# A two-layer MLP's first product by one level of Strassen's scheme, on one core

## The chip, the cores and the metric

One core of a Trainium2 chip runs the whole kernel. The metric is the device time of one execution in microseconds. The engines are TensorE (PE, its weight loads PEld), VectorE (DVE), ScalarE (ACT), GpSimd (POOL) and SyncE (SP), which here only issues DMAs.

## The reference

q, k, v are 8 x 8 x 576 x 64 (batch, head, token, feature) and phi is 8 x 8 x 576 x 32. A softmax of phi over the tokens condenses k and v to 32 memories per head; each token attends to them. The heads side by side give x, 4608 x 512. Two MLPs follow:

```python
x = attention(q, k, v, phi)                    # 4608 x 512
r = np.maximum(x @ w_in1, 0); x = (s * r * r + b) @ w_out1
r = np.maximum(x @ w_in2, 0); out = (r * r) @ w_out2
```

Each w_in is 512 x 2048 and each w_out 2048 x 512. The weights are 64-bit floats in DRAM, the rest 32-bit.

## The kernel before

**Products in three parts.** Each operand is split in two float32r tiles, the cast of it and what the cast leaves, and a product is three matmuls: high by high, high by low, low by high. A cast is an ACT instruction and the remainder a DVE subtraction.

**The first MLP** (lines 568 to 661) runs with the attention over the 8 batches in half-batches of 288 tokens. A step is one half-batch and one of 16 tiles of 128 hidden features: `h1` (line 447) makes 6 matmuls of 288 columns, `x1` (line 469) 12. `h1` is two steps ahead. The attention is a generator of which `slot` runs a piece after so many slots. The result goes to the DRAM tiles `x1d`, transposed (features by tokens).

**Weights.** `narrow` (line 102) makes 32-bit floats of a piece of 64-bit weights: a multiplication on ACT (line 121) and three bit operations on DVE (lines 122 to 125). From step `SPILL` (66), every eighth step takes one of 16 pieces of w_in2 and w_out2 and writes it to DRAM (`wi2d`, `wo2d`, 0.5 MB each, line 132), at a priority behind the step's own work.

**The hand-over.** In the last batch `early` (line 551) opens the buffers of the second MLP, splits half of w_in2 (line 528) and loads and splits the first 512 tokens of x (line 532).

**The second MLP** (lines 666 to 737) runs over 9 blocks of 512 tokens and 16 hidden tiles f, with `h2` (line 672) two steps ahead. `h2` makes 12 matmuls of 512 columns into one bank of `ps_h` (4 feature tiles by 3, line 678), then ACT takes the Relu out of the bank, DVE squares it, ACT casts it and DVE subtracts (lines 683 to 686). Then 4 x 3 matmuls with wo2, 512 columns each, add to four banks of `ps_a` that stay for the block (line 726). `piece` (line 698) splits the other half of w_in2, and wo2, two pieces a step during the first block. At f = 4 the next block of x is loaded, at f = 8 split. After the last f each bank is copied (ACT or DVE) and stored.

The order of the work is the program's, as a list scheduler places it by priority on each engine's queue; each queue runs in order. A tile's buffer is given out again once all that use it are done.

Of the kernel before, what the change touches and what calls it, by code (L numbers as in the profile page):

```python
# [20 lines left out]
def memory_attention_then_two_relu2_mlps(  # L21
# [36 lines left out]
    NB2 = 512  # L58
    NBLK2 = NT // NB2
# [15 lines left out]
    ps_a = ctx.enter_context(tc.tile_pool(name="ps_a", bufs=4, space=PSUM))  # L75
    ps_h = ctx.enter_context(tc.tile_pool(name="ps_h", bufs=2, space=PSUM))
    ps_m = ctx.enter_context(tc.tile_pool(name="ps_m", bufs=2, space=PSUM))
    dram = ctx.enter_context(tc.tile_pool(name="dram", bufs=1, space=DRAM))
    x1d = [dram.tile([P, ND, XG], F32, name=f"x1d{i}") for i in range(NT // XG)]
    wi2d = [dram.tile([P, ND, 512], F32, name=f"wi2d{n}") for n in range(NV)]  # L80
# [10 lines left out]
    def narrow_later(src, kind, dst):  # L91

        narrow_todo.append((src.rearrange("(i p) f -> p i f", i=2), kind, dst))

    def narrow_load(n=1, later=30):
        for src, kind, dst in [narrow_todo.pop(0) for _ in range(min(n, len(narrow_todo)))]:
            with tc.high_priority(-later) if later else ExitStack():
                t = w64_p.tile([P, 2, 512], I64, tag="t", name="wt")
                nc.sync.dma_start(t, src)
            loaded.append((t, kind, dst))  # L100

    def narrow(n=1):
# [5 lines left out]
        for _ in range(n):  # L108
# [5 lines left out]
            with tc.high_priority(-100 if kind == "spill" else -10):  # L114
# [5 lines left out]
                with tc.issue_after(st["act"].ins) if kind == "spill" else ExitStack():  # L120
                    nc.scalar.mul(xf, hw.bitcast(F32), 2.0 ** -112)  # L121
# [9 lines left out]
                elif kind == "spill":  # L131
                    nc.sync.dma_start(dst[0], xf)

# [386 lines left out]
    wi2, xs, early_pools, early_split = [], {}, [], []  # L520
# [11 lines left out]
    def load_x(i):  # L532
        xs_p = early_pools[1]
        t0 = i * NB2
        xh = xs_p.tile([P, ND, NB2], F32R, tag="xh", name="xh")
        xl = xs_p.tile([P, ND, NB2], F32R, tag="xl", name="xl")
        xs[i] = xh, xl
        x = xs_p.tile([P, ND, NB2], F32, tag="x", name="x", bufs=1)
        a = t0
        while a < t0 + NB2:  # L540
            n = min(t0 + NB2 - a, XG - a % XG)
            nc.sync.dma_start(x[:, :, a - t0:a - t0 + n], x1d[a // XG][:, :, a % XG:a % XG + n])
            a += n

        def split():
            for d in range(ND):
                nc.scalar.copy(xh[:, d], x[:, d])
                nc.vector.tensor_tensor(out=xl[:, d], in0=x[:, d], in1=xh[:, d], op=ALU.subtract)
        return split

    def early():
        p2 = ctx.enter_context(tc.tile_pool(name="w2", bufs=1))
        early_pools.extend([p2, ctx.enter_context(tc.tile_pool(name="xs", bufs=2))])
        wi2.extend(p2.tile([P, ND, 2, 512], F32R, name=f"wi2_{n}") for n in range(NV // 2))
        held = []

        def piece(n, d):
            def go():
                if held:
                    held.pop(0)()  # L560
                if n is not None:
                    held.append(split_w(wi2[n][:, d], wi2d[n][:, d]))
                elif d == 0:
                    held.append(load_x(0))
            return go
        early_split.extend([piece(n, d) for n in range(NV // 2) for d in range(ND)] + [piece(None, 0), piece(None, 1)])
# [55 lines left out]
    for i in range(-AHEAD, len(steps)):  # L622
        if i >= 0:
# [13 lines left out]
            if i == SPILL:  # L637
                for n in range(NV):
                    for d in range(0, ND, 2):
                        narrow_later(w_in2[d * P:d * P + 2 * P, n * 512:n * 512 + 512], "spill", [wi2d[n][:, d:d + 2]])  # L640
# [8 lines left out]
        if b == B - 1 and early_split:  # L649
# [13 lines left out]
    right.close()  # L663


    late_p = ctx.enter_context(tc.tile_pool(name="late", bufs=1, side="right"))
    wi2.extend(late_p.tile([P, ND, 2, 512], F32R, name=f"wi2_{n}") for n in range(NV // 2, NV))
    wo2 = late_p.tile([P, NF, 2, DM], F32R, name="wo2")
    gp = ctx.enter_context(tc.tile_pool(name="gp2", bufs=4, side="right"))
    tmp = ctx.enter_context(tc.tile_pool(name="tmp2", bufs=2, side="right"))  # L670

    def h2(i, f):
        hps = ps_h.tile([P, 512], F32, tag="h", name="hps")
        n = 0
        for d in range(ND):
            w = wi2[f // 4][:, d, :, (f % 4) * P:(f % 4) * P + P]
            for wi, xi in ((0, 0), (0, 1), (1, 0)):
                nc.tensor.matmul(hps[:, :NB2], lhsT=w[:, wi], rhs=xs[i][xi][:, d],  # L678
                                 start=(n == 0), stop=(n == 3 * ND - 1))
                n += 1  # L680
        r = tmp.tile([P, NB2], F32, tag="r", name="r")
        g = [gp.tile([P, NB2], F32R, tag=f"g{i}", name=f"g{i}") for i in range(2)]
        nc.scalar.activation(r, hps[:, :NB2], AF.Relu)  # L683
        nc.vector.tensor_tensor(out=r, in0=r, in1=r, op=ALU.mult)  # L684
# [4 lines left out]
    outv = out.rearrange("(b p j) d -> b j p d", b=B, j=J)  # L689
    steps = [(i, f) for i in range(NBLK2) for f in range(NF)]  # L690

    pieces = [(wo2[:, f], wo2d[f // 2][:, f % 2]) for f in range(NF)]
    more = [(wi2[n][:, d], wi2d[n][:, d]) for n in range(NV // 2, NV) for d in range(ND)]
    for n, p in enumerate(more):
        pieces.insert(3 + 2 * n, p)
    held = []
# [6 lines left out]

    for _ in range(3):
        piece()
    for i in range(-AHEAD, len(steps)):
        if i + AHEAD < len(steps):
            gs[i + AHEAD] = h2(*steps[i + AHEAD])
        if i < 0:
            continue  # L710
        blk, f = steps[i]
        if held or pieces:
            piece()
            piece()
        if f == 4 and blk + 1 < NBLK2:
            x_split = load_x(blk + 1)
        if f == 8 and blk + 1 < NBLK2:
            x_split()
        if f == 0:
            acc = [ps_a.tile([P, 512], F32, tag="a", name="oacc") for _ in range(NB2 // P)]  # L720
            o = [ost.tile([P, ND * NB1], F32, tag="o", name="oo") for _ in range(2)]
            o = [o[t // 2][:, t % 2 * DM:t % 2 * DM + DM] for t in range(NB2 // P)]
        g = gs.pop(i)
        for t in range(NB2 // P):
            for n, (xi, wi) in enumerate(((0, 0), (0, 1), (1, 0))):
                nc.tensor.matmul(acc[t], lhsT=g[xi][:, t * P:t * P + P], rhs=wo2[:, f, wi],  # L726
                                 start=(f == 0 and n == 0), stop=(f == NF - 1 and n == 2))
            if f == NF - 1:
                if t % 2:
                    nc.vector.tensor_copy(o[t], acc[t])  # L730
                else:
                    nc.scalar.copy(o[t], acc[t])

                for z in range(2):
# [33 lines left out]
```

## Time and profile before

| what | value |
|---|---|
| time, median of 3 runs | 1573.13 us (1572.85 to 1573.28) |
| span of the profiled execution | 1572.9 us |
| TensorE busy | 1544.8 us, 98% |
| DVE busy | 672.7 us, 43% |
| ACT busy | 692.9 us, 44% |
| DMA | 118.06 MB, mean 75 GB/s |
| second MLP, first to last matmul | 771.47 to 1568.13 us |

The span runs from the first to the last instruction of one profiled execution; its own time is that span, and no other time is given for it. A busy TensorE only says that some matmul was in flight, so how dense the matmuls are is read from the chain in time (how long so many took).

### The profile page before, as it was taken

The numbers are of one execution on the slowest core, as the hardware profiler recorded it, in microseconds if no ns is written. First come the engines' busy times: TensorE is split into PE (matmuls) and PEld (weight loads), VectorE is DVE, ScalarE is ACT, GpSimd is POOL, SyncE is SP. The second block draws the span as 40 slices with busy tenths as digits, with TensorE's granted clock in tenths as the row PEclk, the third lists the DMA queues.
The fourth block names the chain that finished last, engine by engine and source line by source line (L and its number), as shares of the span: only waits on it lengthen the run. The fifth ranks groups of instructions, "written<-read, shape, count | busy, mean of one in ns | idle before, by whom it ended". The sixth has DMA issues, their size and how long they took to land.

```text
span 1572.9 us, 25769 instructions
## 1 busy us (share of the span) xinstructions
PE 1544.8 (98%) x10816; PEld 1343.2 (85%) x10816; DVE 672.7 (43%) x1168; ACT 692.9 (44%) x1467; POOL 1.0 (0%) x7
## 2 busy tenths in 40 slices
PE   5899999999999999999999999999999999999998
PEld 4789989999898999989988888888888888888887
DVE  6985545556555564443353223232323223232222
ACT  4677555656656665576543222222322222222221
POOL 0000000000000000000000000000000000000000
PEclk8999999999999999999999999999999999999999
DMA  9764414344153522032130101020200101010100
GB/s 298 229 193 141 124 59 123 94 154 144 62 180 98 176 82 77 26 97 69 56 108 27 27 1 54 0 54 0 54 1 27 27 1 54 1 28 0 27 1 27
DMA packets 105300, 118.06 MB, mean 75 GB/s; under 512 B 42208, under 2 KB 82144, under 8 KB 105184
## 3 DMA queue, kind: packets, MB, share of 16 engines
q1 hardware_dynamic: 104864, 115.89, 23.8%
q8 instruction: 85, 1.39, 0.4%
q10 hardware_dynamic: 320, 0.52, 0.1%
q14 instruction: 31, 0.25, 0.1%
HBM read 86.77 MB, written 29.62 MB: 74 GB/s over the span
## 4 chain that ended last, share of the span: by engine, by line
PE 95%; DVE 2%; DMA 1%; ACT 1%; issue 0%; SPq 0%; ACTq 0%; DVEq 0%
PE hps L678 25%; PE oacc L726 25%; PE acc L474 25%; PE hps L457 13%; PE vps L426 2%; PE sp L322 1%; PE kvs L239 1%; PE qps L307 1%; PE pp L350 1%; DMA kv<-in_v_dram 0%; DMA wt<-in_moe_w_in_dram 0%; DMA wt<-in_moe_w_out_dram 0%; DVE wx L123 0%; DVE pm L194 0%; ACT wx L121 0%
## 5 line engine op out<-in xcount | busy, mean ns | idle before, releaser
L474 PE MATMUL acc<-g,wo 128*128 128x288 f32 (+1 forms) x3072 | 464.6, 297 | 0.5 <-DVE wo L130 0.3
L474 PEld LDWEIGHTS acc<-g,wo 128*128 128x128 f32 x3072 | 422.4, 188 | 23.3 <-ACT r L464 11.7
L726 PE MATMUL oacc<-wo,g 128*128 128x512 f32 x1728 | 419.6, 392 | 0.0
L726 PEld LDWEIGHTS oacc<-wo,g 128*128 128x128 f32 x1728 | 324.3, 188 | 73.4
L678 PE MATMUL hps<-xh,wi 128*128 128x512 f32 x1152 | 384.1, 394 | 0.0
L684 DVE TENSOR_TENSOR r<-r 128x512 f32<-128x512 f32 x144 | 99.7, 693 | 444.6 <-ACT r L683 444.6
L683 ACT ACTIVATE r<-hps 128x512 f32<-128x512 f32 x144 | 86.0, 597 | 460.9 <-PE hps L678 460.9
L457 PE MATMUL hps<-pt,vp 128*128 128x288 f32 x1536 | 257.1, 300 | 1.5 <-DVE pt L360 0.8
L678 PEld LDWEIGHTS hps<-xh,wi 128*128 128x128 f32 x1152 | 216.1, 188 | 49.5
L457 PEld LDWEIGHTS hps<-pt,vp 128*128 128x128 f32 x1536 | 220.2, 190 | 12.4 <-issue 7.5
L678 PE MATMUL hps<-xl,wi 128*128 128x512 f32 x576 | 225.4, 391 | 0.0
L466 DVE TENSOR_TENSOR g<-r,g 128x288 fp32r<-128x288 f32 x256 | 116.6, 456 | 230.7 <-ACT g L465 228.1
L463 ACT ACTIVATE r<-hps 128x288 f32<-128x288 f32 x256 | 105.2, 411 | 182.2 <-PE hps L457 179.8
L686 DVE TENSOR_TENSOR g<-r,g 128x512 fp32r<-128x512 f32 x144 | 99.6, 692 | 84.5 <-ACT g L685 84.5
L685 ACT CAST g<-r 128x512 fp32r<-128x512 f32 x144 | 89.4, 621 | 94.9 <-DVE r L684 93.8
L678 PEld LDWEIGHTS hps<-xl,wi 128*128 128x128 f32 x576 | 108.1, 188 | 25.1
L464 ACT ACTIVATE r<-r 128x288 f32<-128x288 f32 x256 | 113.7, 445 | 7.0
L465 ACT CAST g<-r 128x288 fp32r<-128x288 f32 x256 | 110.5, 432 | 6.3
L432 DVE TENSOR_TENSOR vp<-vps,vp 128x512 fp32r<-128x512 f32 x64 | 41.6, 686 | 13.0 <-ACT vp L431 12.5
L431 ACT CAST vp<-vps 128x512 fp32r<-128x512 f32 x64 | 34.6, 587 | 15.8 <-PE vps L426 15.7
L121 ACT ACTIVATE wx<-wt 128x1024 f32<-128x1024 f32 x32 | 36.8, 1150 | 10.4 <-DMA wt<-in_moe_w_in_dram 8.2
L123 DVE SCALAR_TENSOR_TENSOR wx<-wt,wx 128x1024 int32<-128x1024 int32 x32 | 39.2, 1224 | 0.8
(224 smaller groups left out, 681.1 us busy)
## 6 DMA issues: line engine op xcount, KB each, us to landing
wt<-in_moe_w_in_dram SPq DMA_DIRECT2D x16, 1024.0 KB, 6.1
wt<-in_moe_w_out_dram SPq DMA_DIRECT2D x16, 1024.0 KB, 6.0
q<-in_q_dram SPq DMA_DIRECT2D x72, 128.0 KB, 3.3
x1d<-xo SPq DMA_DIRECT2D x16, 576.0 KB, 3.5
kv<-in_k_dram SPq DMA_DIRECT2D x23, 384.0 KB, 4.6
kv<-in_v_dram SPq DMA_DIRECT2D x23, 384.0 KB, 5.1
out_dram<-oo SPq DMA_DIRECT2D x68, 128.0 KB, 2.3
x<-x1d SPq DMA_DIRECT2D x6, 1024.0 KB, 5.4
```

The lines of the kernel that those rows point to most:

```text
L457: nc.tensor.matmul(hps[:, :NB1], lhsT=w[:, wi], rhs=pt[xi][:, hp, t0:t0 + NB1], start=(i == 0), stop=(i == 5))
L463: nc.scalar.activation(r[:, :NB1], hps[:, :NB1], AF.Relu)
L464: nc.scalar.activation(r[:, :NB1], r[:, :NB1], AF.Square)
L465: st["act"] = nc.scalar.copy(g[0][:, :NB1], r[:, :NB1])
L466: st["dve"] = nc.vector.tensor_tensor(out=g[1][:, :NB1], in0=r[:, :NB1], in1=g[0][:, :NB1], op=ALU.subtract)
L474: nc.tensor.matmul(acc[d][:, :n], lhsT=wo1[:, f, wi, d * P:d * P + P], rhs=g[xi][:, :n], start=(first and i == 0), stop=(store is not None ...
L678: nc.tensor.matmul(hps[:, :NB2], lhsT=w[:, wi], rhs=xs[i][xi][:, d], start=(n == 0), stop=(n == 3 * ND - 1))
L683: nc.scalar.activation(r, hps[:, :NB2], AF.Relu)
L684: nc.vector.tensor_tensor(out=r, in0=r, in1=r, op=ALU.mult)
L685: nc.scalar.copy(g[0], r)
L686: nc.vector.tensor_tensor(out=g[1], in0=r, in1=g[0], op=ALU.subtract)
L726: nc.tensor.matmul(acc[t], lhsT=g[xi][:, t * P:t * P + P], rhs=wo2[:, f, wi], start=(f == 0 and n == 0), stop=(f == NF - 1 and n == 2))
```

## The change

x @ w_in2 is computed on halves of its three dimensions: 512 features in two halves, 2048 hidden features in two, and a pair of token halves of 384. Seven products of halves replace eight. The sums that they need are made once for the weights and once per pair for x:

- `combine` takes a narrowed piece of w_in2 (all 512 features, 128 columns of each hidden half), makes four sums by DVE, splits the seven operands by ACT and DVE, and writes both parts of all seven to DRAM (`wcd[u]`, 1.84 MB), for 8 units u. It takes the place of 8 of the 16 pieces written every eighth step; each is loaded by four DMAs.
- `load_x` loads 768 tokens of x; its seven steps make the sums and split them, for the first pair in the last batch, later in the pair before.
- `load_unit` streams the weights of one unit from DRAM in two DMAs, into two buffers each, for every pair again.
- `unit` makes the seven products of one unit, 6 matmuls of 384 columns each, in three banks: product 0 into a, 1 into b, 2 on top of a, 3 into c, 4 on top of a, 5 on top of c, 6 on top of a. ACT copies the banks after 0, 2 and 3; DVE adds those copies to the banks after 1, 4 and 5, and clamps and squares. The first token half goes on to wo2 at once, as six groups of three 512-column matmuls, one behind each product of the next unit. The second half is stored in 16 tiles `rd`.
- After the eight units of a pair the 16 tiles are cast (`ready`, two ahead) and taken to wo2, three groups each; the groups of the last two tiles go into the next pair's first unit.
- The three PSUM pools close after the first MLP, and one pool of 8 banks takes their place. wo2 still loads by `piece`, twice per unit.

```diff
+    TP = 384
+    NPAIR = NT // (2 * TP)
+    NU = NF // 2
...
+    wcd = [dram.tile([P, 7, 2, 2, P], F32, name=f"wcd{u}") for u in range(NU)]
...
+                if kind == "combine":
+                    flat = t.rearrange("p i f -> p (i f)")
+                    for d in range(ND):
+                        nc.sync.dma_start(flat[:, d * 2 * P:d * 2 * P + 2 * P].rearrange("p (h c) -> p h c", h=2), src[d])
...
+    def combine(xf, dst):
...
+        q4 = xf.rearrange("p i f -> p (i f)").rearrange("p (d h c) -> p d h c", d=ND, h=2)
+        a11, a12, a21, a22 = [q4[:, 2 * kh:2 * kh + 2, fh, :] for fh in range(2) for kh in range(2)]
+        sums = wst.tile([P, 4, 2, P], F32, tag="x", name="ws")
+        s2, s1, s3, s4 = [sums[:, i] for i in range(4)]
+        for out, in0, in1, op in ((s1, a21, a22, ALU.add), (s2, s1, a11, ALU.subtract),
+                                  (s3, a11, a21, ALU.subtract), (s4, a12, s2, ALU.subtract)):
+            nc.vector.tensor_tensor(out=out, in0=in0, in1=in1, op=op)
+        first = w64_p.tile([P, 4, 2, 2, P], F32R, tag="t", name="wc0")
+        second = w64_p.tile([P, 3, 2, 2, P], F32R, tag="t", name="wc1")
+        plain = q4[:, :, 0, :].rearrange("p (e k) c -> p e k c", e=2)
+        for w, part, of in ((first, slice(0, 2), plain), (first, slice(2, 4), sums[:, 0:2]),
+                            (second, slice(0, 2), sums[:, 2:4]), (second, 2, a22)):
+            nc.scalar.copy(w[:, part, 0], of)
+            nc.vector.tensor_tensor(out=w[:, part, 1], in0=of, in1=w[:, part, 0], op=ALU.subtract)
+        nc.sync.dma_start(dst[:, 0:4], first.bitcast(F32))
+        nc.sync.dma_start(dst[:, 4:7], second.bitcast(F32))
...
+    def load_unit(n):
...
+        for i, (a, b) in enumerate(((0, 4), (4, 7))):
+            t = wc_p.tile([P, b - a, 2, 2, P], F32, tag=f"wc{i}", name=f"wc{i}", bufs=2)
+            nc.sync.dma_start(t, wcd[n % NU][:, a:b])
+            ring[n, i] = t.bitcast(F32R)
...
+        b11, b12, b21, b22 = [x[:, 2 * kh:2 * kh + 2, th * TP:th * TP + TP] for kh in range(2) for th in range(2)]
...
+        def split(e, of):
+            xc = xs_p.tile([P, 2, 2, TP], F32R, tag=f"xc{e}", name=f"xc{e}")
+            nc.scalar.copy(xc[:, 0], of)
+            nc.vector.tensor_tensor(out=xc[:, 1], in0=of, in1=xc[:, 0], op=ALU.subtract)
...
+            t1 = less(b12, b11)
+            split(3, t1)
+            yield
+            t2 = less(b22, t1)
+            split(2, t2)
...
+    psx.close()
...
+    ps = ctx.enter_context(tc.tile_pool(name="ps", bufs=8, space=PSUM))
...
+        def product(e, to, start):
+            n = 0
+            for k in range(2):
+                for wi, xi in ((0, 0), (0, 1), (1, 0)):
+                    nc.tensor.matmul(to[:, :TP], lhsT=w[e // 4][:, e % 4, wi, k], rhs=xc[e][:, xi, k],
+                                     start=(start and n == 0), stop=(n == 5), skip_group_check=True)
+                    n += 1
+            return to[:, :TP]
...
+        def added(t, of, to):
+            nc.vector.tensor_tensor(out=t, in0=of, in1=to, op=ALU.add)
+            nc.vector.scalar_tensor_tensor(out=t, in0=t, scalar=0.0, in1=t, op0=ALU.max, op1=ALU.mult)
+
+        p1 = copied(product(0, a, True))
+        yield
+        r = tmp.tile([P, TP], F32, tag="r", name="r")
+        added(r, product(1, b, True), p1)
+        low = cast(r)
+        yield
+        u2 = copied(product(2, a, False))
+        yield
+        c = bank("pc")
+        p5 = copied(product(3, c, True))
+        yield
+        added(rd[NU + u], product(4, a, False), p5)
+        yield
+        added(rd[u], product(5, c, False), u2)
+        yield
+        r = tmp.tile([P, TP], F32, tag="r", name="r")
+        nc.scalar.activation(r, product(6, a, False), AF.Relu)
+        nc.vector.tensor_tensor(out=r, in0=r, in1=r, op=ALU.mult)
+        high = cast(r)
+        groups.extend(block(p, 0, u, low, u == 0, False))
+        groups.extend(block(p, 0, NU + u, high, False, u == NU - 1))
...
+            if n + 1 < NPAIR * NU and n > 0:
+                load_unit(n + 1)
+            if u == 4 and p + 1 < NPAIR:
+                part = load_x(p + 1)
+            for w, _ in enumerate(unit(p, u)):
+                take()
+                if w in (1, 4) and (held or pieces):
+                    piece()
...
+        take(3)
+        for f in fs:
+            ready(f + 2)
+            if f % 2 and p + 1 < NPAIR:
+                next(part, None)
+            if f < NF - 2 or p + 1 == NPAIR:
+                take(6 if f == 0 else 3)
```

## Rows read from the trace of the kernel before

**Rows 1.** The page: busy time of the engines; clock granted in 40 slices.

```profile
PE 1544.8 (98%) x10816; PEld 1343.2 (85%) x10816; DVE 672.7 (43%) x1168; ACT 692.9 (44%) x1467; POOL 1.0 (0%) x7
...
PEclk8999999999999999999999999999999999999999
```

**Rows 2.** The page: chain that ended last, by engine, by line.

```profile
PE 95%; DVE 2%; DMA 1%; ACT 1%; issue 0%; SPq 0%; ACTq 0%; DVEq 0%
PE hps L678 25%; PE oacc L726 25%; PE acc L474 25%; PE hps L457 13%; PE vps L426 2%; PE sp L322 1%; PE kvs L239 1%; PE qps L307 1%; PE pp L350 1%; DMA kv<-in_v_dram 0%; DMA wt<-in_moe_w_in_dram 0%; DMA wt<-in_moe_w_out_dram 0%; DVE wx L123 0%; DVE pm L194 0%; ACT wx L121 0%
```

**Rows 3.** Windows, second MLP: stretch, length, engines' busy us, PEclk, DMA share, GB/s.

```profile
771.30:859.90 88.60, 88.60 (x387) 72.20 (x386) 41.35 (x63) 36.17 (x63) 0.00 (x0) 1.00 0.26 80
859.90:948.40 88.50, 88.50 (x386) 72.02 (x385) 25.82 (x39) 22.65 (x38) 0.00 (x0) 1.00 0.09 24
```

**Rows 4.** Chain in time, second MLP: start us, us, engine, tile, line, count.

```profile
771.47 8.18 PE hps L678 x36
...
804.43 2.75 PE hps L678 x12
...
809.93 2.80 PE hps L678 x12
812.74 2.76 PE oacc L726 x12
...
1559.92 8.21 PE oacc L726 x36
```

**Rows 5.** Chain in time, first MLP.

```profile
412.37 0.80 PE hps L457 x6
413.17 1.59 PE acc L474 x12
...
474.30 0.39 PE acc L474 x3
```

**Rows 6.** Groups by form, ACT and DVE: busy us, mean ns of one, idle before.

```profile
L465 ACT CAST g<-r 128x288 fp32r<-128x288 f32 x256 | 110.5, 432 | 6.3
...
L685 ACT CAST g<-r 128x512 fp32r<-128x512 f32 x144 | 89.4, 621 | 94.9 <-DVE r L684 93.8
...
L221 DVE TENSOR_TENSOR ph<-ph,t 128x384 f32<-128x384 f32 x24 | 11.9, 548 | 1.1 <-PE t L216 1.1
...
L314 ACT COPY qT<-qps 128x384 f32<-128x384 f32 x23 | 10.9, 474 | 5.2 <-PE qps L307 5.1
```

**Rows 7.** Timeline where the second MLP starts: start us, us, instruction, idle before.

```profile
771.60 1.13 ACT L528 CAST wo<-wx 128x512 fp32r<-128x512 f32 x2
...
772.25 1.29 DVE L529 TENSOR_TENSOR wo<-wx,wo 128x512 fp32r<-128x512 f32 x2 [0.16 <-ACT wo L528]
```

**Rows 8.** Groups by form, narrowing the weights: busy us, mean ns.

```profile
L123 DVE SCALAR_TENSOR_TENSOR wx<-wt,wx 128x1024 int32<-128x1024 int32 x32 | 39.2, 1224 | 0.8
...
L121 ACT ACTIVATE wx<-wt 128x1024 f32<-128x1024 f32 x32 | 36.8, 1150 | 10.4 <-DMA wt<-in_moe_w_in_dram 8.2 <-DMA wt<-in_moe_w_out_dram 2.2
...
L122 DVE TENSOR_SCALAR wx<-wx 128x1024 int32<-128x1024 int32 x32 | 22.0, 692 | 13.6 <-ACT wx L121 13.1
```

**Rows 9.** Window at the kernel's start, columns as in rows 3.

```profile
0.00:40.00 40.00, 24.19 (x301) 19.16 (x302) 26.09 (x46) 17.56 (x41) 0.95 (x7) 0.87 0.92 298
```

**Rows 10.** The page: DMA issues, KB each, us to landing.

```profile
x<-x1d SPq DMA_DIRECT2D x6, 1024.0 KB, 5.4
...
x<-x1d SPq DMA_DIRECT2D x2, 768.0 KB, 5.5
```

**Rows 11.** Window in which w_in2 is narrowed, columns as in rows 3.

```profile
262.00:440.00 178.00, 177.83 (x1720) 166.52 (x1719) 100.67 (x187) 112.19 (x260) 0.00 (x0) 1.00 0.40 126
```

**Rows 12.** Timeline of batch 3's k and v loads.

```profile
347.84 0.50 SPq L177 DMA_DIRECT2D kv<-in_v_dram  x1
...
350.90 0.91 PE L239 MATMUL kvs<-kv,e 64*32 64x128 f32 x47 [0.17 <-DMA kv<-in_v_dram]
```

**Rows 13.** The page: weight loads of the first MLP's second product.

```profile
L474 PEld LDWEIGHTS acc<-g,wo 128*128 128x128 f32 x3072 | 422.4, 188 | 23.3 <-ACT r L464 11.7
```

More of the change, by code (lines that the diff above doesn't have):

```diff
@@ L539, in load_x @@
+    def load_x(p):
+        xs_p = early_pools[0]
+        t0, t1 = p * 2 * TP, (p + 1) * 2 * TP
+        x = xs_p.tile([P, ND, 2 * TP], F32, tag="x", name="x")
         a = t0
-        while a < t0 + NB2:
-            n = min(t0 + NB2 - a, XG - a % XG)
+        while a < t1:
+            n = min(t1 - a, XG - a % XG)
             nc.sync.dma_start(x[:, :, a - t0:a - t0 + n], x1d[a // XG][:, :, a % XG:a % XG + n])
             a += n
[L545 to L548, printed above, removed]
@@ L569, in memory_attention_then_two_relu2_mlps @@
+        return steps()
+    def early():
+        early_pools.append(ctx.enter_context(tc.tile_pool(name="w2", bufs=1)))
+        part = load_x(0)
+        load_unit(0)
+        load_unit(1)
+        early_split.extend([lambda: next(part, None)] * 7)
     load_phi(0)
@@ new lines, in memory_attention_then_two_relu2_mlps, with block, group, go @@
+    accs = {}
+    def block(p, half, f, g, first, last):
+        def group(t):
+            def go():
+                if first:
+                    accs[half, t] = bank("oacc")
+                acc = accs[half, t]
+                gg = g() if callable(g) else g
+                for n, (xi, wi) in enumerate(((0, 0), (0, 1), (1, 0))):
+                    nc.tensor.matmul(acc, lhsT=gg[xi][:, t * P:t * P + P], rhs=wo2[:, f, wi],
+                                     start=(first and n == 0), stop=(last and n == 2))
+                if last:
+                    store(p, half, t, acc)
+            return go
+        return [group(t) for t in range(TP // P)]
@@ new lines, in memory_attention_then_two_relu2_mlps, with store @@
+    room = []
+    def store(p, half, t, acc):
+        if t != 1:
+            room[:] = [ost.tile([P, ND * NB1], F32, tag="o", name="oo")]
+        o = room[0][:, t % 2 * DM:t % 2 * DM + DM]
+        if t % 2:
+            nc.vector.tensor_copy(o, acc)
+        else:
+            nc.scalar.copy(o, acc)
+        for z in range(2):
+            grp = ((2 * p + half) * TP + t * P) // 64 + z
+            eng = nc.scalar if (z and p == NPAIR - 1 and half) else nc.sync
+            eng.dma_start(outv[grp // J, grp % J], o[64 * z:64 * z + 64])
@@ L698, in piece @@
+    held, split_of = [], {}
+    pieces = [(wo2[:, f], wo2d[f // 2][:, f % 2]) for n in range(NU) for f in (n, NU + n)]
     def piece():
@@ L702, in piece, with take @@
             held.pop(0)()
+    def take(n=1):
+        for _ in range(min(n, len(groups))):
+            groups.pop(0)()
     for _ in range(3):
         piece()
[L706 to L734, printed above, removed]
-                    grp = (blk * NB2 + t * P) // 64 + z
-                    eng = nc.scalar if (z and blk == NBLK2 - 1) else nc.sync
-                    eng.dma_start(outv[grp // J, grp % J], o[t][64 * z:64 * z + 64])
```

129 lines of the change are left out of this document (70 added, 59 removed).

## The prediction

> **What bounds the kernel now.** I read the page from the top. TensorE is busy 98% of the span at full granted clock [rows 1], but a busy TensorE need not be a full one, so the chain of waits comes next: 95% of the path to the end is matmuls, and half of it is the second MLP, in equal parts x @ w_in2 (line 678) and g @ w_out2 (line 726) [rows 2]. Then that stage by itself: in windows of one 512-token block, 88.5 us long, TensorE is busy 88.5, ACT 22.7, DVE 25.8, DMA a tenth; the clock is 1.00, that is its 2.4 GHz level. In the first block wo2 and half of wi2 are still read and split, DMA at three times the share, and it takes 88.6 us: nothing on another engine shows [rows 3]. The chain in time gives the price of a matmul. It runs from 771.47 to 1568.13 without a hole: 796.66 us for 2 x 1728 matmuls of 512 columns, 230.5 ns each. Line 726 takes 2.76 us for 12, and 8.21 for 36 at the end (2.74); line 678 takes 2.75 or 2.80 for 12 [rows 4]. I put line 726 at 2.755, thus 144 x 2.755 = 396.7 us, and line 678 at the other 400.0 us. So whatever takes columns from TensorE here is worth its full time, as long as nothing else gets late.
>
> **Part 1, the products.** Removed: 9 x 16 x 12 = 1728 matmuls of 512 columns. Added: 6 pairs x 8 units x 7 products x 6 = 2016 of 384. Columns fall by exactly 1/8 (884,736 to 774,144); matmuls rise by 288. No row has a 384-column matmul, so I bound it. In the first MLP, 18 matmuls of 288 columns take 0.80 + 1.59 us, 132.8 ns each, and three alone to a bank 0.39, so short groups cost nothing extra [rows 5]. The line through 132.8 at 288 and 230.5 at 512 (0.436 ns a column, 7 ns fixed) gives 174.7 ns at 384. Ends: 384/512 of 229.2 is 171.9, 384/288 of 132.8 is 177.1. I take the line, since 384 lies between two measured widths. 2016 x 174.7 = 352.2 us (346.6 to 357.0), against 400.0: **-47.8 us** (-53.4 to -43.0).
>
> The Trainium skill, TensorE: Matmul & The Clock Gate, section Back-to-back issue gap, gives N/2.4 + 2.5 ns for an isolated warm matmul: 215.8 at 512 and 162.5 at 384, and a gain of 45.3 us. The rows are 7% above it at 512 and 8% at 288 (122.5 by the page), so I stay with the line.
>
> Line 726 becomes groups of three matmuls of the same 512 columns, still 1728: no change.
>
> **Part 2, the engines behind the products.** Of the ACT and DVE work in the second MLP nothing is on the path while TensorE stays dense; its cover is the unit, 42 x 174.7 + 18 x 229.6 ns (2.755 us / 12) = 11.47 us. ACT: four reads of a 384-column bank at 0.474 us (the COPY of that shape) and two casts at 0.51 (between 0.432 at 288 and 0.621 at 512): 2.9 us. DVE: three adds, three clamp-and-squares, one square, two subtractions, nine at 0.548: 4.9 us [rows 6]. Neither is half full. What counts is the hand-over of a bank. Bank a holds products 0, 2, 4, 6, bank c holds 3 and 5, and each may be added to only after its reader is done. The tightest is product 4: ACT copies bank a after product 2, but on ACT's queue that copy stands behind the cast of the low half, which waits for two DVE operations on product 1. Counted from the end of product 1, with at most 0.16 us for a signal, a subtraction's wait on its cast [rows 7]: DVE from 0.16 to 1.26, cast from 1.42 to 1.93, copy to 2.40, seen by TensorE at 2.57. Product 4 starts after three groups of 0.69 and products 2 and 3 at 1.05, at 4.17. Slack 1.6 us. The others are products 2, 5 and 6, which wait for one read of about 0.5 us with a product and two groups between: 1.05 + 1.38. So zero, while the groups stand between.
>
> They don't in the very first unit, when no group exists yet. There, too, ACT and DVE have just stored the last x1 tile and split two pieces of wo2 for 1.13 and 1.29 us [rows 7], and the accumulators are one new pool over the three old ones, which can hold product 0 until the last store is read. Product 2 and product 4 then come up some 0.5 us short each: **+1 us** (0 to 3).
>
> At the end of a pair TensorE has three groups, 2.07 us, before it needs the cast of the first stored tile. If that cast is issued behind the last unit's own chain (read 0.47, square 0.55, cast 0.51, then itself 0.51 and 0.55) it comes at 2.6 to 3.1. It need not be, since those tiles are ready long before and ACT is idle there. Six pairs, 0 to 1 us each: **+2 us** (0 to 6). In that phase 9 matmuls (2.07 us) cover one cast and one subtraction per tile, begun two tiles ahead, and every second tile brings a step of the next pair's splits (768 columns, a cast and one or two subtractions), below the rows of 1024 columns, 1.15 on ACT and 1.22 on DVE, or twice that on DVE [rows 8]; the dearest pair of tiles asks 2 x 0.55 + 2.45 = 3.6 of DVE's 4.1 us: nothing.
>
> **Part 3, the weight stream.** A unit needs 7 x 2 x 2 x 128 floats per partition, 1.84 MB, 48 times, two DMAs each; removed are 16 loads of wi2 pieces and the loads of x in blocks of 512 tokens. Per 11.47 us that is 160 GB/s. The start of the kernel moves 298 GB/s over 40 us [rows 9]; the nearest single transfers take 5.4 us (1024 KB) and 5.5 (768 KB) [rows 10]. Even one after the other they fit, 10.9 of 11.47, and each has the ring's second buffer: the first DMA of unit n+1 can go when product 3 of unit n-1 is done, some 15 us early. The x load of a pair (1.57 MB at unit 4, on the same SP queue) costs 11 us so counted, and the last pair-phase without loads (33 us) pays it back. On SP the output stores stand between loads only once per half. Zero, from 0 to what rival B says. Its cover gone, each late microsecond counts 48 times.
>
> **Part 4, the first MLP.** Eight pieces that before cost ACT 1.15 and DVE 3.1 us (1.224 twice and 0.69) [rows 8] get four sums, four casts and four subtractions: about +2.3 on ACT and +4.2 on DVE each, and write 1.84 MB instead of 0.5 MB. In 262 to 440 us, where they run, DVE is busy 101 of 178 us and ACT 112; +34 and +18 leave a quarter of each free, under a TensorE that is full [rows 11]. But the k and v loads are just in time there: issued at 347.84, waited for 0.17 us at 350.90 [rows 12]. They share SP's queue with the new stores and with three more load issues per piece. A store that sits ahead of them for 5.4 us at both batches of that stretch is the upper end. **+2 us** (0 to 11).
>
> The end is as before: the copy and the store of the last tile.
>
> **The sum.** The span, 1572.9 us, is 0.2 below the median of the three runs, 1573.13, so I count from the median: 1573.1 - 47.8 + 1 + 2 + 2 = 1530.3, say 1530.
>
> **Rivals.**
> A, slower: the hand-overs are exposed. If a bank's reader and its next writer come to stand side by side on TensorE, by the order that the scheduler writes or because ACT's copies queue behind casts, each of the four per unit costs a copy and a signal each way, 0.47 + 2 x 0.16 = 0.79 us: 48 x 4 x 0.79 = 152 us, 1682. It decides at (47.8 - 5) / 48 = 0.9 us per unit; with 0.5 it gives 1554. Against it: 1.6 us of slack at the tightest place, and ACT and DVE under half full. 0.11, of that 0.05 beyond the break-even.
> B: the weights come late. It needs under 160 GB/s; at 140, 13.1 us per unit, 48 x 1.6 = 79 us, 1609. For it: 160 GB/s has to be held where this stage now moves 24 [rows 3]. Against: 298 at the start [rows 9]. 0.04.
> C: the combining holds up the first MLP, 11 us instead of 2: 1539. For it, the k and v loads without slack; against, the free quarter of DVE. 0.10.
> D: the price is per matmul, not per column. If every weight load were paid in full, 288 more at 188 ns are +54.1 against -48.2 for the columns (110,592 at 0.436), with the 5 us of waits 1584. It decides at (48.2 - 5) / 288 = 150 ns a matmul. The row speaks against it: a whole matmul of 288 columns takes 132.8 ns, less than its 188 ns load [rows 5, 13]. 0.01. The Trainium skill, the same page, section The mechanism, says that a weight load overlaps a running matmul only where the row group differs, which here it never does; by that rule D would hold, and the row contradicts it.
> E: the change doesn't shorten the path at all, gains and waits cancel: 1573, 0.01.
>
> **How the numbers follow.** Forecast 0.73, A 0.11, B 0.04, C 0.10, D 0.01, E 0.01. The forecast's own range is 1520 (the low end of the products, no wait) to 1541 (the high end with 3, 6 and 2); C ends within it, and part of A reaches to 1548. 1519 to 1548 leaves out most of A, B, D and E, under 2 in 10. 0.2%, some 3 us, is about what a measurement of this kernel can tell from no change. Faster: forecast, C, 0.06 of A, 0.01 of B, 0.90. Same: 0.01 of B and E, 0.02. Slower: 0.05 of A, 0.02 of B, D, 0.08.
>
> **What would show it.** Right: the second MLP's chain still without holes, 42 matmuls of a unit in 7.3 us, 750 us in all, and clock 1.00. Part 2 wrong: TensorE waiting on ACT's copies or DVE's adds inside a unit. Part 3 wrong: TensorE waiting on the weights' DMA. Part 4 wrong: the second MLP starting later than 771.5 us by more than 2. The prediction falls if a 384-column matmul takes over 177 ns, or if a unit takes over 12 us.

## The result and the profile after

The changed kernel takes 1535.08 us (median of 4 runs, 1533.77 to 1535.55); in the same session the kernel before takes 1573.01 (1572.85 to 1573.28). The ratio is 0.9755, with an interval from 0.9742 to 0.9769. The forecast was 1530. The profiled execution took 1534.62 us, 1.8 of it outside the span.

The page of the changed kernel: its busy times and chain (span 1532.8 us), which answer to [rows 1, 2], and the weight stream's DMAs:

```profile
PE 1497.5 (98%) x11104; PEld 1372.5 (90%) x11104; DVE 810.0 (53%) x1480; ACT 723.5 (47%) x1591; POOL 1.0 (0%) x7
...
PE oacc L794 25%; PE acc L504 25%; PE pa L747 13%; PE hps L487 12%; PE pc L747 7%; PE pb L747 3%; PE vps L456 2%; DMA kv<-in_v_dram 1%; PE sp L352 1%; PE kvs L269 1%; PE qps L337 1%; DMA wt<-in_moe_w_in_dram 1%; PE pp L380 1%; ACT xc L585 0%; DVE wx L131 0%
...
wc<-wcd SPq DMA_DIRECT2D x48, 1024.0 KB, 5.1
wc<-wcd SPq DMA_DIRECT2D x48, 768.0 KB, 4.3
```

TensorE is as busy as before, 98%, with fewer columns. The products (pa, pc, pb on line 747) hold 23% of a shorter chain where x @ w_in2 held 25%. DVE went from 672.7 to 810.0 us, still about half.

The chain in time at the start of the second MLP, answering to [rows 4]: start, length, tile, count.

```profile
771.48 4.38 PE acc L504 x33
...
775.88 0.60 ACT xo L538
...
776.96 1.29 PE pa L747 x6
778.25 1.04 PE pb L747 x6
779.29 1.04 PE pa L747 x6
...
797.14 0.69 PE oacc L794 x3
...
808.62 0.69 PE oacc L794 x3
...
865.51 1.34 ACT xc L585 x2
...
866.86 0.52 ACT g L733
...
867.43 30.92 PE oacc L794 x135
```

Four things are to be seen. Six matmuls of 384 columns take 1.04 us (1.05 between groups). A unit takes 11.48 us, from 797.14 to 808.62. Between the last x1 matmul and the first product TensorE stands for 1.1 us. And at the end of a pair it waits for ACT. Inside a unit the chain has no hole, and the window from 776.9 to 865 us has the granted clock at 1.00.

The waits of the changed kernel: TensorE's from 200 to 776 us, TensorE's from 776 us to the end, and one of SP's queue from 200 to 776 us (line and what waits, releaser, total us, times, longest).

```profile
PE kvs L269 <- DMA kv<-in_v_dram: 4.4, 2, 2.5
...
PE oacc L794 <- ACT g L733: 2.0, 5, 0.4
PE pa L747 <- ACT xo L538: 0.7, 1, 0.7
...
SPq L161 <- DVE wc L160: 50.0, 5, 17.4
```

TensorE waits nowhere on the weight stream. It waits for v loads, 4.4 us; in the kernel before it was 0.17 us in this stretch, once [rows 12]. SP stood 50 us at line 161, the store of a combined piece, until DVE had made it.

**Where the time went.** I number the runs of 12 matmuls on the first MLP's second product (line 474 before, 504 after) from 0 to 255 and take the starts of their first matmuls from the trace.

| stretch (us) | before | after | difference |
|---|---|---|---|
| start to step 24 | 126.09 | 124.97 | -1.12 |
| steps 72 to 160 (w_in2 is combined) | 251.36 | 257.34 | +5.98 |
| the other x1 steps, to the last x1 matmul | 393.72 | 393.64 | -0.08 |
| last x1 matmul to the last of all | 796.55 | 751.82 | -44.73 |

They add up to -39.95, and the spans differ by 40.1. The first line says little: no edit of the kernels below acts before step 68, and in their traces step 24 began anywhere between 123.68 and 125.92 us. The profiled execution of before was a long one (by some 2 us, as shown further down), so the medians differ by less, by 37.9.

The second MLP did what was forecast (-47.8 + 1 + 2 = -44.8). The first MLP lost 6 us where 2 were forecast, and that is the question of the experiments.

The timeline of SP's queue and of TensorE in the changed kernel, with one line of DVE, at batch 3's and batch 4's k and v loads: start, length, instruction, and in brackets the idle time before it and its releaser.

```profile
342.37 0.39 SPq L206 DMA_DIRECT2D kv<-in_k_dram  x1
...
344.95 0.34 SPq L161 DMA_DIRECT2D wcd<-wc  x1
...
345.19 0.70 DVE L160 TENSOR_TENSOR wc<-ws,wc 128x512 fp32r<-128x512 f32 x1
...
345.92 0.34 SPq L162 DMA_DIRECT2D wcd<-wc  x1
346.31 1.22 SPq L207 DMA_DIRECT2D kv<-in_v_dram  x1
...
354.14 0.91 PE L269 MATMUL kvs<-kv,e 64*32 64x128 f32 x47 [2.49 <-DMA kv<-in_v_dram]
...
436.02 0.39 SPq L206 DMA_DIRECT2D kv<-in_k_dram  x1
...
439.88 1.23 SPq L207 DMA_DIRECT2D kv<-in_v_dram  x1
...
447.23 0.91 PE L269 MATMUL kvs<-kv,e 64*32 64x128 f32 x47 [1.93 <-DMA kv<-in_v_dram]
```

Between a k load and its v load stand the two stores of a combined piece (lines 161 and 162). The second is issued only when DVE's last subtraction (345.19 to 345.89) is done. So the v load goes 3.9 us after its k load; in the kernel before the same pair went out 0.42 us apart (343.17 and 343.59).

The chain in time has the landing of these loads, and some matmuls right behind the second stall: start, length, what; first the kernel before, at batch 3, then the changed one, at batches 3 and 4.

```profile
343.17 0.37 SPq L176
...
343.59 7.17 DMA kv<-in_v_dram
```

```profile
346.31 7.70 DMA kv<-in_v_dram
...
439.88 7.22 DMA kv<-in_v_dram
...
449.41 1.44 PE hps L487 x6
```

Both kernels' loads take over 7 us to land here, in the changed kernel with 1.84 MB of stores issued just ahead. That too is part of the wait, as the second experiment shows.

The second stall has a tail. A window behind it: stretch, length, engines' busy time, granted clock, DMA share, GB/s.

```profile
448.00:452.00 4.00, 4.00 (x45) 3.98 (x30) 2.39 (x4) 1.12 (x5) 0.00 (x0) 0.57 1.03 398
```

After TensorE stood for 1.93 us, the mean granted clock from 448 to 452 is 0.57: the records have it at the lower level, 1.2 GHz, for 3.4 us from 448.5. What that costs can be read from the starts of the steps. From step 108 to step 140, where the second stall lies, the changed kernel loses 3.4 us to the kernel before, and its wait is 1.9 of them. The run with token halves of 256 below, whose first MLP is the same, has a wait of 1.92 us there and no low clock, and loses 1.9. So the low clock costs 1.5 us. The 6.0 us of the table are then 0.3 up to step 100, which no wait explains, 2.3 at the first stall (2.49 less the 0.17 of before), 1.9 and 1.5.

### The profile page after: what moved, and what is told of

It reads as the page before. It is cut to its first block, busy times and chain, and to the rows that moved or that the text cites. A ratio compares the mean times of both kernels' runs of the same rounds, so it can differ in the third digit from the quotient of the medians.

```text
span 1532.8 us, 27085 instructions
## 1 busy us (share of the span) xinstructions
PE 1497.5 (98%) x11104; PEld 1372.5 (90%) x11104; DVE 810.0 (53%) x1480; ACT 723.5 (47%) x1591; POOL 1.0 (0%) x7
## 4 chain that ended last, share of the span: by engine, by line
PE 92%; DVE 3%; DMA 2%; ACT 2%; issue 1%; SPq 0%; ACTq 0%; DVEq 0%
PE oacc L794 25%; PE acc L504 25%; PE pa L747 13%; PE hps L487 12%; PE pc L747 7%; PE pb L747 3%; PE vps L456 2%; DMA kv<-in_v_dram 1%; PE sp L352 1%; PE kvs L269 1%; PE qps L337 1%; DMA wt<-in_moe_w_in_dram 1%; PE pp L380 1%; ACT xc L585 0%; DVE wx L131 0%
## 5 line engine op out<-in xcount | busy, mean ns | idle before, releaser
L747 PE MATMUL pa<-xc,wc 128*128 128x384 f32 x1152 | 226.0, 336 | 0.7 <-ACT xo L538 0.7
L747 PEld LDWEIGHTS pa<-xc,wc 128*128 128x128 f32 x1152 | 205.5, 188 | 13.6 <-ACT xo L538 0.9
L747 PE MATMUL pc<-xc,wc 128*128 128x384 f32 x576 | 116.5, 337 | 0.0
L747 PEld LDWEIGHTS pc<-xc,wc 128*128 128x128 f32 x576 | 103.7, 188 | 8.0
L733 ACT CAST g<-r 128x384 fp32r<-128x384 f32 x96 | 49.2, 512 | 111.4 <-DVE r L759 86.9
L734 DVE TENSOR_TENSOR g<-rd,g 128x384 fp32r<-128x384 f32 x96 | 52.5, 557 | 93.2 <-ACT g L733 93.1
L733 ACT CAST g<-rd 128x384 fp32r<-128x384 f32 x96 | 48.3, 515 | 109.7 <-PE oacc L794 109.7
L734 DVE TENSOR_TENSOR g<-r,g 128x384 fp32r<-128x384 f32 x96 | 53.5, 558 | 48.5 <-ACT g L733 48.5
L754 ACT COPY s<-pa 128x384 f32<-128x384 f32 x96 | 45.9, 478 | 32.5 <-PE pa L747 30.8
L747 PE MATMUL pb<-xc,wc 128*128 128x384 f32 x288 | 58.3, 337 | 0.0
```

Source lines behind the costliest of these rows:

```text
L733: nc.scalar.copy(g[0], r)
L734: nc.vector.tensor_tensor(out=g[1], in0=r, in1=g[0], op=ALU.subtract)
L747: nc.tensor.matmul(to[:, :TP], lhsT=w[e // 4][:, e % 4, wi, k], rhs=xc[e][:, xi, k], start=(start and n == 0), stop=(n == 5), skip_group_c ...
L754: nc.scalar.copy(t, of)
```

## The experiments

Theory Q says that the first MLP's loss comes from the order of SP's queue: a store that waits for DVE holds the v load behind it. Its rivals are that the stores' bytes crowd out the loads (W), and that the work for the sums on ACT and DVE makes something late (rival C's place). For the second MLP the experiments take up rivals A, B and D. The kernel before, run beside the first four kernels on one chip, took 1573.17 us (1571.49 to 1573.82); beside the other four it took 1573.17 too (1570.81 to 1574.31).

**The stores on POOL's queue.** All else is kept.

```diff
-        nc.sync.dma_start(dst[:, 0:4], first.bitcast(F32))
-        nc.sync.dma_start(dst[:, 4:7], second.bitcast(F32))
+        nc.gpsimd.dma_start(dst[:, 0:4], first.bitcast(F32))
+        nc.gpsimd.dma_start(dst[:, 4:7], second.bitcast(F32))
```

> The two stores of each combined weight piece go to the idle POOL queue instead of SP; nothing else changes. Theory Q (queue): in the changed kernel the v load of batch 3 was issued at 346.31 us and that of batch 4 at 439.88, 3.4 to 3.5 us after the k load before it, because SP stood at a store that waited for DVE; TensorE then came up 3.65 and 4.05 us late. So both waits fall to some 0.2 us as before the change, the clock step at 448.5 us goes, and the second MLP starts about 5.8 us earlier, near 770 us; time about 1529. Rival W (wires): the loads land late because the DMA engines are full of the 14.7 MB of stores; the bytes are the same here, so the waits stay at 3 to 4 us each and the time at 1535. Second MLP unchanged at 751 to 752 us for both.

Measured: 1535.34 us (1531.77 to 1538.11), ratio 0.976 (0.9743 to 0.9777), as the changed kernel. The waits for v are gone, but steps 72 to 160 take 258.04 us, 0.7 more. The timeline shows the new wait:

```profile
453.21 1.13 ACT L129 ACTIVATE wx<-wt 128x1024 f32<-128x1024 f32 x1 [3.06 <-DMA wt<-in_moe_w_out_dram]
...
458.36 0.27 ACT L322 COPY vmT<-kvt 128x128 f32<-128x128 f32 x1 [1.55 <-DVE kb L321]
...
458.68 0.74 PE L337 MATMUL qps<-ident,q 128*128 128x128 f32 x3 [3.00 <-ACT vmT L322]
```

ACT stands for the next piece's load, which came late (its buffer is one of two that now also hold the combined operands until they are stored; the load was issued at 445.37, 0.14 us after the store of 439.27 had landed); DVE's copy (line 321, 457.75) is behind that piece, ACT's vmT behind the copy, and TensorE waits 3.00 us (5.0 in three waits). The records then have the clock at 1.2 GHz for 3.4 us from 458.9. So taking the stores off SP does away with the waits for v, as Q says: both v loads go out 0.4 us behind their k loads and land in 4.1 us. But the stall moved to ACT's queue, and the time is not the 1529 that Q forecast. This does not rule W out, since the large stores now also come after the v loads.

**Only the place in the queue.** The large stores go on POOL's queue, and in their old places on SP stand stores of 16 columns. By the trace these wait for ACT's cast of the same operands and not for DVE's last subtraction (343.86 to 344.58), so they hold a v load somewhat less.

```diff
-        nc.sync.dma_start(dst[:, 0:4], first.bitcast(F32))
-        nc.sync.dma_start(dst[:, 4:7], second.bitcast(F32))
+        nc.gpsimd.dma_start(dst[:, 0:4], first.bitcast(F32))
+        nc.sync.dma_start(tiny[0], first.bitcast(F32)[:, 0, 0, 0, 0:16])
+        nc.gpsimd.dma_start(dst[:, 4:7], second.bitcast(F32))
+        nc.sync.dma_start(tiny[1], second.bitcast(F32)[:, 0, 0, 0, 0:16])
```

> As the run before, but SP gets two stores of 16 columns each (8 KB) per piece into a scratch tile at the places where the large ones stood, with the same waits for DVE; the large ones stay on POOL. Theory Q: SP stands again at the same two places, so the v loads of batches 3 and 4 go out about 3.4 us late and TensorE waits 3 to 4 us twice: 1534 to 1535, 5 to 6 us over the run before. Rival W: the small stores move nothing, so the time equals that of the run before.

Measured: 1535.53 us (1534.36 to 1538.9), ratio 0.976 (0.9744 to 0.9776). By time that is the run before over again, and not 5 to 6 us more, as Q had it. Timeline of SP, POOL's queue and TensorE at batch 3, then at batch 4:

```profile
341.06 0.38 SPq L210 DMA_DIRECT2D kv<-in_k_dram  x1
343.35 0.32 SPq L166 DMA_DIRECT2D tiny<-wc  x1
...
343.90 0.53 POOL L163 DMA_DIRECT2D wcd<-wc  x1 [23.17 <-DVE wc L160]
344.03 0.38 SPq L211 DMA_DIRECT2D kv<-in_v_dram  x1
...
351.64 0.91 PE L273 MATMUL kvs<-kv,e 64*32 64x128 f32 x47 [3.00 <-DMA kv<-in_v_dram]
```

```profile
436.76 0.38 SPq L210 DMA_DIRECT2D kv<-in_k_dram  x1
...
439.35 0.43 SPq L211 DMA_DIRECT2D kv<-in_v_dram  x1
...
439.64 0.54 POOL L163 DMA_DIRECT2D wcd<-wc  x1 [23.12 <-DVE g L500]
```

The landing of the two v loads: the first by the chain in time, the second by its source line.

```profile
344.03 7.47 DMA kv<-in_v_dram
```

```profile
DMA to landing us min/median/max: 4.0/4.0/4.0
```

Both v loads stand behind a store of 8 KB, 3.0 and 2.6 us after their k loads. TensorE waits 3.00 us for the first and not at all for the second. What differs is the landing. At batch 3 a large store went out on POOL 0.13 us ahead of the v load, which landed in 7.47 us; at batch 4 it went out 0.29 us behind, and the load landed in 4.0. With 4.0 us the first load, too, would have been there in time, at 348.0, since TensorE stood still from 348.64 on.

So the place in the queue is not enough: neither Q nor W alone makes the wait. The same sum holds in the changed kernel. TensorE stood from 351.65 and from 445.30, and the v loads issued at 346.31 and 439.88 would have been there at 350.4 and 444.0 with the 4.1 us that they took in the run before. Nor is a slow landing enough: in the kernel before 7.17 us cost 0.17, because the load went out right behind its k load. In the changed kernel the two stores do both, they hold the v load and they are in flight ahead of it. That it is their bytes that lengthen the landing is argued from these cases; no run holds the loads with the large stores left out.

The wait on vmT is there too (3.2 us), and steps 72 to 160 take 262.40 us: both stalls, each with a stretch of low clock (3.4 us from 352.8, 6.8 from 458.6).

**The groups behind their unit.** Rival A tried on purpose: the seven products side by side, the six groups after them.

```diff
             for w, _ in enumerate(unit(p, u)):
-                take()
+                if w == 0:
+                    ready6 = len(groups)
                 if w in (1, 4) and (held or pieces):
                     piece()
+            take(ready6)
```

> The six groups of matmuls with wo2 come behind the unit's seven products instead of one between each two; everything else as in the changed kernel. It takes away the cover of the hand-overs of banks a and c. Rival A of the prediction (hand-overs exposed when reader and next writer stand side by side): 0.79 us at each of four hand-overs, up to 48 x 4 x 0.79 = 152 us, 1687; half of it where a product between hides half. Theory H: one product of 1.05 us between reader and writer is cover enough, as in the first unit of the changed kernel, whose seven products follow each other in 1.04 us steps with no group between; then 1535, at most 3 us over.

Measured: 1529.39 us (1528.26 to 1530.24), ratio 0.9723 (0.9708 to 0.9737), 5.7 us under the changed kernel. Its chain in time:

```profile
838.06 4.10 PE oacc L794 x18
...
848.42 1.06 PE pa L747 x6
849.48 4.10 PE oacc L794 x18
```

A unit is 11.42 us. The 0.06 us are gained in the products and not in the groups: behind a group a product's first three matmuls take 174, 176 and 182 ns from start to start, behind another product 173 or 174 (medians of 41 units), and here one product of a unit stands behind a group instead of six. The pair-end wait is gone. From 776 us to the end TensorE waits once, 1.2 us at 821 us, where ACT's copy (line 754) stood behind a cast of wo2 whose load was late. From the last x1 step to the end it takes 747.86 us instead of 751.82. Rival A's mechanism does not bite at this size: one product between a bank's reader and its next writer is cover enough without any group (product 6 begins 0.22 us after DVE's addition from its bank is done, in the median unit), and the interleaving costs 4 us (48 units of 0.06 and the pair ends' 2.0, less the 1.2).

**Token halves of 256.** One size changed: nine pairs instead of six, 256-column products, the weights streamed half again as fast.

```diff
-    TP = 384
+    TP = 256
...
-        take(3)
+        take(TP // P)
```

> Token halves of 256 instead of 384: 9 pairs in place of 6, so 3024 products' matmuls of 256 columns in place of 2016 of 384, 72 weight units streamed in place of 48 (132 MB in place of 88), and a unit of about 42 x 0.119 + 12 x 0.2296 = 7.75 us, so 237 GB/s in place of 160. By the line through 132.8 ns at 288 and 174.2 at 384 (0.431 ns a column, 8.7 fixed) a matmul of 256 columns takes 119.0 ns: 3024 x 119.0 = 359.9 against 351.2 us, and three more pair ends of 0.4: about 1545 if the stream keeps up. Rival B of the prediction (weights late): if the transfers of a unit go one after the other (5.1 + 4.3 us as in the changed kernel) a unit takes 9.4 us and TensorE waits 1.65 us in each, 72 x 1.65 = 119 us: 1664, with waits on the weights' DMA. Rival D (price per matmul): 120 ns would be exceeded clearly, 1008 more matmuls at up to 188 ns.

Measured: 1554.91 us, one run, 10 above the expectation. The chain in time of a unit, and the window from 780 to 920 us:

```profile
814.70 0.70 PE oacc L794 x3
...
820.35 0.72 PE pc L747 x6
821.07 1.60 PE pa L747 x12
822.67 0.70 PE oacc L794 x3
```

```profile
780.00:920.00 140.00, 139.05 (x887) 124.48 (x886) 77.61 (x179) 52.12 (x129) 0.00 (x0) 1.00 0.70 235
```

Six matmuls take 0.71 us, 118 ns each, as the prediction's line says for 256 (0.436 x 256 + 7 = 119). No wait on weights appears at 235 GB/s, so rival B is far off at 160. D falls: a matmul is well below its 188 ns load [rows 13]. The excess is in the unit, 7.97 us here (814.70 to 822.67) and 7.93 in the median, where 42 x 0.119 + 12 x 0.2296 = 7.75. After product 5, twelve matmuls (product 6 and the next product 0) take 1.60 us where two products of 0.71 would be 1.42: here product 6 follows product 5 with no group between, and the longest waits that the profile names inside the second MLP are a product's on DVE's addition (line 758), 1.2 us in four. The starts show the rest. In the median unit product 6 begins 0.05 us after that addition is done, where the run before has 0.22; its first matmul comes 150 ns after product 5's last, and its second 222 ns after its first, where 120 is usual. That is 0.13 of the 0.18 us. So this is rival A's mechanism, at a cover of one product of 0.71 us.

**The changed kernel again**, beside the kernels that follow.

> The changed kernel once more, unaltered, on the chip of the next three runs: 1535 within 1.5 us, k and v waits of 3 to 4 us in batches 3 and 4 again (v loads sent some 3.4 us after their k load), second MLP from the last x1 matmul to the last matmul 751.8 us. It is the measure for the three that follow.

Measured: 1535.08 us (1531.82 to 1535.39), ratio 0.9754 (0.9741 to 0.9767). The v waits are there again (4.6 us in two), steps 72 to 160 take 257.44 us.

**The pieces two or four steps away from the loads.** If the loss comes from where a piece meets a batch's loads, the pieces should go where no loads are. The edit with 6; the other has 4 in its place.

```diff
-        if i in (-1, 1, 3, 6, 8, 12, 15, 18, 20, 23, 26, 28, 30) or i >= SPILL and i % 8 == 0:
+        if i in (-1, 1, 3, 6, 8, 12, 15, 18, 20, 23, 26, 28, 30) or i >= SPILL and i % 8 == 6:
```

> The weight pieces are taken at steps 6 of every eight instead of 0; bytes, instructions and queues stay. In the program's order on SP the two stores of the colliding pieces now stand before the k and v loads of batches 3 and 4 and not between k and v. Theory Q (the loads wait on SP behind a store that waits for DVE): both waits of TensorE for the v load go, no clock step there, the first MLP ends 5 to 6 us earlier, 1529 to 1530. Theory S (slots: the two 8 KB buffers are now held until a piece is stored, so a piece's load is late and some in-order queue stalls wherever the piece stands, as ACT did with the stores on POOL): the k and v waits go, but a stall of 3 us or more turns up at another place, on ACT or on SP, and the time stays within 2 us of the changed kernel's. Rival W (DMA engines full): v waits stay.

> As the run before with the pieces at steps 4 of every eight. On SP the stores and the piece's next load then all stand ahead of a batch's k and v loads, two to three steps earlier. Theory Q: again no wait for v, 1529 to 1530. Theory S: a stall somewhere else, 1533 to 1535. If both runs gain alike, the place of the stores is the whole cause; if only one does, it is the place and what else waits there.

Measured: 1531.66 us (1530.33 to 1533.51), ratio 0.9738 (0.9724 to 0.9751), with 6; 1530.94 us (1529.98 to 1533.46), ratio 0.9735 (0.9722 to 0.9748), with 4. What TensorE waited for between 126 us and the second MLP, first with 6, then with 4:

```profile
PE acc L504 <- DVE g L496: 2.3, 1, 2.3
```

```profile
PE acc L504 <- ACT xo L538: 0.5, 2, 0.3
```

With 4, no load is waited for, the records show no low clock between 126 us and the end's last instructions, and steps 72 to 160 take 253.54 us: 2.2 above the kernel before instead of 6.0, with the same work and the same bytes. With 6 the v waits are gone too; one piece then makes DVE late for the first MLP itself, 2.3 us, and the clock is low once, from 358.7 us (255.92). So with 4 most of the loss goes when the stores stand elsewhere, with the same total of bytes and of engine time. How much is less sure. The stage is one execution of each kernel, and with the changed kernel's first MLP it took 255.31 to 257.44 in four executions (the run with token halves of 256 is the lowest, with both waits and no low clock). By the medians, 6 gains 3.4 us and 4 gains 4.1, and the runs overlap (1531.82 to 1535.39 beside these two).

**Both together**: the groups behind their unit, the pieces at 6, and the three old PSUM pools opened in another order, for the wait at the second MLP's start.

> The groups behind the unit's products (which was 6 us under the changed kernel), the weight pieces at steps 6, and the three PSUM pools of the first MLP opened in the order h, m, a instead of a, h, m, so that the first unit's banks lie over those of h and m, which are free before the last x1 store. If the wait of 1.1 us at the start of the second MLP hangs on the banks below, it goes; if it hangs on the closing of the pools, it stays. Second MLP: 747 to 748 us from the last x1 matmul to the last. With theory Q 1523 to 1524, with theory S 1528 to 1529.

Measured: 1526.94 us (1525.76 to 1528.19), ratio 0.9708 (0.9695 to 0.9721), 8.1 us under the changed kernel; this is the fastest version. The second MLP takes 748.10 us, steps 72 to 160 take 254.21. The chain in time where the second MLP starts:

```profile
767.96 3.98 PE acc L504 x30
...
771.97 0.60 ACT xo L538
...
773.05 1.28 PE pa L747 x6
```

The start stays at 1.1 us after the last x1 matmul, though by the order of opening other banks should lie beneath the first accumulator (the traces do not name banks). So the order of the pools made no difference: in either the first product waits for the last readers of the closed pools. A version in which the second MLP uses the old pools was not tried.

## Why the prediction was right, and where it was off

**Part 1, the products: right.** 174.7 ns was forecast for 384 columns; 1.04 to 1.05 us for six are 173.3 to 175. At 256 columns the same line held to a nanosecond. The Trainium skill, TensorE: Matmul & The Clock Gate, section Back-to-back issue gap, gives N/2.4 + 2.5 ns for an isolated warm matmul, that is 162.5 at 384 and 109.2 at 256; the traces are 7 and 9% above it, much as at 512 and 288.

**Part 2, inside a unit: right, with slack to spare.** 11.47 us was forecast, 11.48 measured, with no wait. But the cover was taken to be the groups ("zero, while the groups stand between"), and that was wrong: with the groups behind the unit the products alone cover the readers, and the unit is shorter by 0.06 us. Groups of three 512-column matmuls among 384-column ones were costed at nothing ("no change"); each product behind a group costs some 0.01 us more than one behind a product, which is these 0.06 us.

**The first unit: right size, wrong step.** Products 2 and 4 were said to "come up some 0.5 us short each". They don't: in the changed kernel they start 1.04 us after the product ahead of them, and ACT issued product 2's copy (780.36) ahead of the cast (780.74) that the forecast put before it. What costs is the other half of that paragraph, which had no price of its own: the new pool over the old ones holds product 0 until the last x1 tile is read out. From the start of the last x1 matmul to that of the first product it is 1.01 us instead of 0.13: +0.9.

**Pair ends: right.** 2.0 us in five waits against +2, and the cause is the one named, ACT. It was said that the cast "need not be" behind the unit's chain. It is behind more: the next pair's two x casts (line 585, 865.40 to 866.96) stand on ACT ahead of the g casts.

**Part 3, the weight stream: right.** Zero waits, and none at 235 GB/s either.

**Part 4, the first MLP: the step that failed.** +2 us was taken from a range of 0 to 11; it measured 6.0. By the prediction's own sign this part is wrong: the second MLP starts at 776.96 us, 5.5 later than 771.5. The added work was sized well. The changed kernel's largest group by form for one part of it, DVE's subtractions of the splits (busy us, mean ns, idle before):

```profile
L160 DVE TENSOR_TENSOR wc<-ws,wc 128x512 fp32r<-128x512 f32 x16 | 10.9, 687 | 0.0
```

With the line's other two groups (5.5 and 3.4 us) and the sums (line 153, 32 of 0.42 us) that is some 33 us on DVE, and ACT's casts (line 159) are 18.1 us, against the forecast's 34 and 18. The mechanism, a store ahead of the k and v loads on SP's queue, was named too. Its price was not worked out: the store was weighed by its landing time, 5.4 us, as if it were in the way or not. What counts is two things. The store itself waits, for DVE's last subtraction of a piece, which puts the v load 3.5 us further behind its k load than before (3.94 against 0.42). And the load then lands in 7.7 and 7.2 us, with the stores in flight ahead of it, where 4.1 would have been in time. So both batches stall, for 2.5 and 1.9 us. The prediction also took the wrong issue from [rows 12]: the v load waited for at 350.90 is the one issued at 343.59, not the one at 347.84 (no v load of the kernel before lands in under 3.8 us). And the second stall is followed by a stretch at 1.2 GHz, six hps matmuls in 1.44 us (from 449.41) where six take 0.80 [rows 5], worth 1.5 us that no term of the sum had. Rival C's place was thus the right one, at about half its price of 11 us.

**The sum.** With the measured terms, 1573.1 - 44.7 + 6.0 = 1534.4, against 1535.08. The 0.7 left is below what single starts differ by. The prediction also took the profiled span (1572.9) for one 0.2 us under the median. In nine later executions of the kernel before the spans were 1568.8 to 1572.3, with times 1.7 to 2.1 above them; so the profiled execution was some 2 us longer than the median one.

**Rivals A, B and D.** None came about in the changed kernel: no reader is waited for inside a unit, no weight is late, and the price stays one per column, down to a matmul of 118 ns under weight loads of 188 [rows 13]. The Trainium skill, on the same page, section The mechanism, has the load overlap only where the row group differs, in its list of what overlaps (a sentence above the list also names a background weight buffer); the 256-column products contradict the list once more.

**Open.** With the pieces at 4, 2.2 us of the loss in steps 72 to 160 are left and waits explain 0.5; the rest lies spread over TensorE's instructions, and no run takes it apart. Nor is it separated how much of the two waits for v is the hold in the queue and how much the slow landing.

## What to carry to other kernels

When a step with stores is put into a stretch that is already just in time, price each load by both what the head of its queue waits for and what is in flight ahead of it: here a hold of 2.6 us alone made no wait, a landing of 7.2 us alone made one of 0.17, and both together made waits of 1.9 to 3 us. Moving the step away from the loads, with the work unchanged, was worth some 3 to 4 of the 6 lost microseconds; moving the store to another queue only moved the stall, since the two buffers beneath it were short as well. And a cover that looks necessary should be taken away once: at 384 columns the groups between the products protected nothing and cost 4 us. At 256 columns, with one product as the cover, the hand-over did show.

## What was not expected of the hardware

After a stall of 1.9 to 3.0 us on TensorE the records often show the granted clock at 1.2 GHz for 3.4 us: from 448.5 in the changed kernel, 458.9 with the stores on POOL, 353.8 with the groups behind their unit, 358.7 with the pieces at 6, there 0.2 us before the stall ended; with the small stores on SP it was 6.8 us once, from 458.6. A wait of 1.9 us then costs 3.4. Not every stall did so: the 2.49 us before 354.14 in the changed kernel were followed by none, nor were the 2.06 and 1.92 with token halves of 256, nor the 1.4 us that is left in the last version. A change from a group of 512-column matmuls to a product of 384-column ones cost some 0.01 us, in the product's second and third matmul (176 and 182 ns instead of 173). And the start of the kernel varied by up to 2.4 us between traces, as much as some of the effects here, so a stage is better compared by its own starts, as in the table above, than by the span.
